# Attention products of a run kept together on TensorE, products with v issued for two pieces at a time

## The chip, the cores and the metric

One core of one Trainium2 chip runs the program. The metric is the device time of one launch in microseconds (us); the kernel before was run three times, with 1156.73, 1160.39 and 1160.76 us, median 1160.39. Engines are named as in the profile: PE is TensorE, DVE VectorE, ACT ScalarE, POOL GpSimd, SP SyncE.

## What is computed

Sigmoid attention over 8 batches of 12 heads (448 positions, head dimension 64), and then a two-layer network on the 3584 tokens. Cut to what matters:

```python
scores = q @ k.T / sqrt(64) - log(448)
attn = 1 / (1 + exp(-scores))
x = attn @ v                       # heads side by side: 3584 x 768
h = x @ w_in                       # 768 -> 2048
g = where(h >= 1, h, where(h <= -1, 0, (h + 1)**2 / 4))
out = g @ w_out                    # 2048 -> 768
```

## The kernel before

The data are 32-bit floats. From the ninth pair of heads on, q and k are written as a high and a low half in 16 bits (`hl`, made in `prep_b`), from the fifteenth on v and the attention weights too (`v`, `ahl`), and each product of two such operands is the sum of three 16-bit matmuls: high by high, and the two mixed ones. The weights of the network and its activations are split in the same way.

**Attention.** Two heads form a pair (`p`), and a pair has four pieces (`c`): three blocks of 128 key positions and a last one, the middle piece, with the 64 that are left, in which both heads lie side by side. A piece `i = 4 p + c` goes through four steps:

- `scores` (line 387) makes the piece's scores in a PSUM tile `psc`, of which there are two. Per head one matmul over all 128 rows of the array takes the high half of q and both halves of k (line 409), and one over 64 rows adds the low half of q (line 418). The two matmuls of line 418, one per head, use the upper and the lower half of the array's rows. A middle piece from pair 14 on takes three whole-array matmuls instead (line 404).
- `weigh` applies the sigmoid on ACT in PSUM (line 450), copies the high half out on ACT (line 458) and makes the low half on DVE (line 459). The `psc` tile is free after that.
- `av` (line 466) multiplies with v into `pav` (line 491): six matmuls for a whole piece, four for a middle one. Each gives 64 rows of output, head 0 in the left and head 1 in the right half of the array's columns, and the two heads alternate.
- After a pair's last piece ACT copies `pav` to x (line 500), and DVE takes its largest value (line 501).

In the column of one-row sums, `all_sum` (line 155) adds up the largest values of a later pair in a matmul with 2 or 3 columns; what comes out sets that pair's scales, with which `prep_b` splits it on POOL.

**Network.** For the first two batches the first layer is line 719; from the third on it runs in a block scheme with seven products instead of eight (`up_blocks`, line 685), 128x224 each. The second layer is line 755 for all. During the second batch DVE and ACT also make the weights of the block scheme (`mix` and `unmixed`, lines 625 to 653).

**Order.** `step(i)` issues the scores up to piece `i + 3` and then `av`; up to pair 13 it takes one piece a step, from pair 14 on two pieces every second step. The main loop calls `step` between the units of the network of the batch before, so that attention of batch b + 1 runs within the network of batch b. Inside that, a list scheduler at build time orders each engine's instructions by priority and by when it reckons their operands to be there: the order on PE is not the order of the calls. PE runs it strictly in that order.

At the end of a batch `start_blocks` and `finish_blocks` take the largest x of all (DVE, one PE matmul in line 171, DVE) and split x; the next batch's first layer waits for that.

Of the kernel before, what the change touches and what calls it, by code (L numbers as in the profile page):

```python
# [14 lines left out]
F32 = mybir.dt.float32  # L15
# [3 lines left out]
AF = mybir.ActivationFunctionType  # L19
ALU = mybir.AluOpType  # L20
# [3 lines left out]
P = 128  # L24
# [29 lines left out]
QA = 17  # L54
QT = 3
CORN = 10
TP = 1

DW = 8
# [10 lines left out]
def sigmoid_attention_mlp(ctx: ExitStack, tc: tile.TileContext, first_qvk, qkv, w_in, w_out, out_t):  # L70
# [312 lines left out]

    pieces = {}

    def scores(todo):

        tiles = []
        for i in todo:
            p, c = divmod(i, NPC)  # L390
            mid = c == NKC
            w = slice(c * P, S if mid else (c + 1) * P)
            psc = ps_sc.tile([P, 2, 512], F32, tag="psc", name="psc")
            tiles.append(psc)
            if p < NFULL:
                r = ready[p][0]
                for j in range(2):
                    out = psc[j * D : (j + 1) * D, 0, :S] if mid else psc[:, j, :S]
                    rows = slice(j * D, (j + 1) * D)
                    nc.tensor.matmul(out, r[rows, 2, w], r[rows, 0, :], start=True, stop=True)  # L400
            elif mid and p >= NFULL + NHALF:
                hl = ready[p][4]
                for t, (kh, qh) in enumerate(((0, 0), (1, 0), (0, 1))):
                    nc.tensor.matmul(psc[:, 0, :S], corner(p)[:, kh, :], hl[:, 0, qh, :], start=t == 0, stop=t == 2)  # L404
            else:
                kq = ready[p][0]
                for j in range(2):
                    out = psc[j * D : (j + 1) * D, 0, :S] if mid else psc[:, j, :S]
                    nc.tensor.matmul(out, kq[:, j, 1, w], kq[:, j, 0, :], start=True, stop=False)  # L409
        for i, psc in zip(todo, tiles):  # L410
            p, c = divmod(i, NPC)
            mid = c == NKC
            if p >= NFULL and not (mid and p >= NFULL + NHALF):
                hl, w = ready[p][4], slice(c * P, S if mid else (c + 1) * P)
                for j in range(2):
# [22 lines left out]
    def weigh(i, psc):  # L438
# [5 lines left out]
        sqk = 1.0 / math.sqrt(D) if p < NFULL else ready[p][2][:, 0:1]  # L444
        if p < NFULL + NHALF:
            a32 = att_p.tile([P, 2, S], F32, tag="ahl", name="a32")
            nc.scalar.activation(a32[:, :n, :], a, AF.Sigmoid, bias=nls, scale=sqk)  # L447
# [8 lines left out]
            parts = [(a, ahl[:, 0], ahl[:, 1])]  # L456
        for x, hi, lo in parts:
            nc.scalar.activation(hi, x, AF.Copy, scale=ATT)  # L458
            nc.vector.scalar_tensor_tensor(out=lo, in0=x, scalar=ATT, in1=hi, op0=ALU.mult, op1=ALU.subtract)  # L459
        pieces[i] = ahl  # L460

    state = {"scored": 0}

    def av(i):
        p, c = divmod(i, NPC)
        b, hp = divmod(p, NP)
        if c == 0:
            state["pav"] = ps_av.tile([P, 512], F32, tag="pav", name="pav")
            if hp == 0:
                state["xm"] = sml_p.tile([P, NP], F32, tag="xm", name="xm", bufs=2)  # L470
        pav = state["pav"]
        at = pieces.pop(i)
        mid = c == NKC
        v = ready[p][1]
        split = p >= NFULL + NHALF
        terms = []
        for j in range(2):
            o = slice(j * D, (j + 1) * D)
            full_v = slice((2 * c + j) * D, (2 * c + j + 1) * D)
            if p < NFULL and mid:  # L480
                full_v = slice(2 * c * D, (2 * c + 1) * D)
            if not split:
                r = o if mid else slice(0, P)
                terms.append([(v[r, full_v], at[r, 0 if mid else j, :])])
            elif mid:
                terms.append([(v[:, vh, full_v], at[:, 0, j, :]) for vh in range(2)])
            else:
                terms.append([(v[:, vh, full_v], at[:, ah, j, :]) for vh, ah in ((0, 0), (1, 0), (0, 1))])
        for t in range(len(terms[0])):
            for j in range(2):  # L490
                nc.tensor.matmul(  # L491
                    pav[j * D : (j + 1) * D, :S], *terms[j][t],
                    start=c == 0 and t == 0, stop=mid and t == len(terms[j]) - 1,
                )
# [296 lines left out]
    def step(i):  # L791
# [6 lines left out]
        if c == 2:  # L798
            prep_b(p + 2)
            if late:  # L800
                prep_a(p + 3)
        if i < NPC * (NFULL + NHALF):
# [12 lines left out]


    wi = Weight(w_in, w_in_sb, "wi", [5 + 2 * (f % 6) for f in range(NFC)])
# [152 lines left out]
```

## Time and profile before

| | |
|---|---|
| median of 3 runs | 1160.39 us |
| the profiled execution, as timed | 1159.12 us |
| its span in the trace | 1157.4 us |
| PE matmul busy | 1135.0 us, 98% of the span |
| PE weight loads | 666.1 us, 58%, beside the matmuls |
| DVE busy | 815.8 us, 70% |
| ACT busy | 722.1 us, 62% |
| POOL busy | 294.4 us, 25% |
| mean granted TensorE clock | 0.999 of full speed |

The span is from the first to the last instruction; the launch around it adds 1.7 us. A matmul counts as busy from its start to its modelled end, which lies behind the start of the next one. Where matmuls follow each other closely the time that one costs is therefore read as the distance between two starts, from the timeline, and not from its duration.

### The profile page before, as it was taken

The page shows a single profiled execution, that of the slowest core. Times are in us where ns is not written, and L with a number is a line of the kernel's source. Part 1 is how long each engine was busy: PE and PEld are TensorE (multiplying, and loading weights), DVE is VectorE, ACT ScalarE, POOL GpSimd, SP SyncE. Part 2 cuts the span into 40 slices and gives each one's busy share as a digit, 9 for nine tenths or more (in the row PEclk, how much of TensorE's full clock was granted, in tenths as well). Part 3 has the DMA queues.
Part 4 walks back from the last instruction along what each step waited for, and adds up shares of the span by engine and source line. Part 5 has one row for each costly group of instructions (what it writes and reads, how often), then busy time and mean ns, then how long its engine had stood idle before and what let it go on. Part 6 is the DMA issues. An engine that isn't in the chain of part 4 may idle for free.

```text
span 1157.4 us, 20215 instructions
## 1 busy us (share of the span) xinstructions
PE 1135.0 (98%) x7662; PEld 666.1 (58%) x7662; DVE 815.8 (70%) x1730; ACT 722.1 (62%) x1199; POOL 294.4 (25%) x367
## 2 busy tenths in 40 slices
PE   8899999999999999999999999999999999999998
PEld 2234334444446775567745785457854677558954
DVE  6988886879987895468936787367964589646820
ACT  6978888578666784557754786447764576423410
POOL 0000000001542354324523353325344233210000
PEclk9999999999999999999999999999999999999999
DMA  9943443162564654225632465224742165203300
GB/s 366 380 138 135 143 165 97 50 212 105 192 209 144 239 211 127 76 94 205 219 102 65 145 207 203 66 66 147 264 145 76 53 207 200 100 17 123 133 22 27
DMA packets 58112, 170.00 MB, mean 147 GB/s; under 512 B 8608, under 2 KB 39840, under 8 KB 51872
## 3 DMA queue, kind: packets, MB, share of 16 engines
q1 hardware_dynamic: 56288, 159.29, 39.9%
q10 hardware_dynamic: 1728, 9.44, 2.3%
q8 instruction: 60, 0.98, 0.3%
q14 instruction: 36, 0.29, 0.1%
HBM read 126.94 MB, written 23.40 MB: 130 GB/s over the span
## 4 chain that ended last, share of the span: by engine, by line
PE 76%; DMA 8%; DVE 6%; ACT 4%; POOL 3%; issue 1%; SPq 0%; POOLq 0%; DVEq 0%; ACTq 0%
PE po L755 30%; PE ph L685 23%; PE pav L491 8%; PE ph L719 7%; DMA raw<-qkv 4%; PE psc L409 3%; PE psc L418 3%; DMA w_out_sb<-w_in 2%; PE psc L404 1%; DVE ahl L459 1%; ACT psc L450 1%; POOL hl L373 1%; DVE mixa L625 1%; ACT dump L335 1%; POOL raw L371 1%
## 5 line engine op out<-in xcount | busy, mean ns | idle before, releaser
L755 PE MATMUL po<-ghl,w_out_sb 128*128 128x448 f16 x2304 | 446.9, 353 | 1.8 <-ACT ghl L735 1.8
L755 PEld LDWEIGHTS <-w_out_sb 128*128 128x128 f16 x2304 | 221.5, 98 | 217.2 <-issue 17.6
L685 PE MATMUL ph<-w_in_sb 128*128 128x224 f16 x3024 | 307.7, 259 | 1.7 <-DMA w_in_sb<-blocks 1.3
L685 PEld LDWEIGHTS <-w_in_sb 128*128 128x128 f16 x3024 | 282.6, 98 | 31.1 <-issue 27.6
L459 DVE SCALAR_TENSOR_TENSOR ahl<-psc,ahl 128x896 f16<-128x896 f32 (+1 forms) x170 | 153.0, 900 | 98.8 <-ACT ahl L458 96.9
L450 ACT ACTIVATE psc<-psc,nls,sqk 128x896 f32<-128x896 f32 (+1 forms) x136 | 129.8, 971 | 94.0 <-PE psc L418 76.1
L371 POOL TENSOR_SCALAR raw<-raw,qkv_s 128x448 f32<-128x448 f32 (+1 forms) x93 | 70.9, 777 | 443.8 <-DVE qkv_i L135 355.7
L458 ACT ACTIVATE ahl<-psc 128x896 f16<-128x896 f32 (+1 forms) x170 | 127.0, 762 | 30.6 <-DVE ahl L459 29.4
L719 PE MATMUL ph<-xhl,w_in_sb 128*128 128x448 f16 x576 | 112.5, 353 | 0.0
L335 ACT ACTIVATE dump<-raw 128x448 f16<-128x448 f32 (+1 forms) x105 | 61.6, 587 | 72.0 <-DMA raw<-qkv 71.3
L694 DVE TENSOR_TENSOR xhl<-ph,xhl 128x224 f32<-128x224 f32 x240 | 87.7, 383 | 26.0 <-PE ph L685 19.6
L491 PE MATMUL pav<-ahl,v 128*64 128x448 f16 x748 | 98.2, 360 | 0.4 <-DVE ahl L459 0.4
L735 ACT ACTIVATE ghl<-g 128x448 f16<-128x448 f32 x128 | 72.5, 572 | 37.2 <-DVE g L734 36.7
L732 ACT ACTIVATE g<-xhl,hr,ihr 128x448 f32<-128x448 f32 x96 | 68.7, 752 | 41.8 <-DVE xhl L694 40.8
L736 DVE TENSOR_TENSOR ghl<-g,ghl 128x448 f16<-128x448 f32 x128 | 84.2, 664 | 8.2 <-ACT ghl L735 7.7
L733 DVE SCALAR_TENSOR_TENSOR g<-g,rk 128x448 f32<-128x448 f32 x112 | 79.8, 727 | 13.9 <-ACT g L732 13.5
L719 PEld LDWEIGHTS <-w_in_sb 128*128 128x128 f16 x576 | 54.8, 98 | 58.2 <-issue 8.9
L373 POOL TENSOR_TENSOR hl<-raw,hl 128x448 f16<-128x448 f32 x62 | 72.8, 1194 | 0.0
L409 PE MATMUL psc<-qk 128*128 128x448 f16 x252 | 66.4, 354 | 2.8 <-ACT a L447 1.8
L734 DVE SCALAR_TENSOR_TENSOR g<-xhl,ihs,g 128x448 f32<-128x448 f32 x96 | 66.3, 708 | 0.3
L768 DVE TENSOR_SCALAR o<-po,od 128x448 f32<-128x448 f32 x42 | 28.5, 679 | 53.1 <-PE po L755 53.1
L430 POOL COPY w_in_sb<-hl 64x128 f16<-64x128 f16 x68 | 32.4, 476 | 127.3 <-DVE hl L367 125.4
(151 smaller groups left out, 1131.6 us busy)
## 6 DMA issues: line engine op xcount, KB each, us to landing
w_in_sb<-blocks SPq DMA_DIRECT2D x48, 1344.0 KB, 6.6
raw<-qkv SPq DMA_DIRECT2D x34, 704.0 KB, 4.8
qk<-hl SPq DMA_DIRECT2D x320, 56.0 KB, 2.0
w_out_sb<-w_in SPq DMA_DIRECT2D x16, 768.0 KB, 11.1
out_t<-o SPq DMA_DIRECT2D x48, 224.0 KB, 1.9
blocks<-mixs SPq DMA_DIRECT2D x8, 768.0 KB, 3.5
w_out_sb<-w_out ACTq DMA_DIRECT2D x6, 768.0 KB, 4.6
raww<-w_out ACTq DMA_DIRECT2D x6, 768.0 KB, 5.8
```

The source lines that it names most:

```text
L371: nc.gpsimd.tensor_scalar(out=rt, in0=rt, scalar1=s[:, t : t + 1], scalar2=1.0, op0=ALU.mult, op1=ALU.mult)
L373: nc.gpsimd.tensor_tensor(out=dst[:, 1, :], in0=rt, in1=hi, op=ALU.subtract)
L409: nc.tensor.matmul(out, kq[:, j, 1, w], kq[:, j, 0, :], start=True, stop=False)
L450: nc.scalar.activation(a, a, AF.Sigmoid, bias=nls, scale=sqk)
L458: nc.scalar.activation(hi, x, AF.Copy, scale=ATT)
L459: nc.vector.scalar_tensor_tensor(out=lo, in0=x, scalar=ATT, in1=hi, op0=ALU.mult, op1=ALU.subtract)
L491: nc.tensor.matmul(pav[j * D : (j + 1) * D, :S], *terms[j][t], start=c == 0 and t == 0, stop=mid and t == len(terms[j]) - 1,)
L685: nc.tensor.matmul(out, w[:, wt, wh, c * P : (c + 1) * P], xc[:, xt, c, xh, :], start=j in (0, 2) and c + wh + xh == 0, stop=c == HC - 1 a ...
L694: add = lambda out, q, other: nc.vector.tensor_tensor(out=out, in0=quarter(q), in1=other, op=ALU.add)
L719: nc.tensor.matmul(ph[:, :S], w_in_sb[:, f, wh, c * P : (c + 1) * P], xhl[:, c, xh, :], start=c == 0 and wh + xh == 0, stop=c == NCC - 1 a ...
L736: (nc.gpsimd if f % GPOOL else nc.vector).tensor_tensor(out=ghl[:, f, 1, :], in0=g, in1=hi, op=ALU.subtract)
L755: nc.tensor.matmul(po[:, :S], w_out_sb[:, f, wh, m * P : (m + 1) * P], ghl[:, f, gh, :], start=f == lo and wh + gh == 0, stop=f == hi - 1 ...
```

## The change

- `chain` gives each run of attention matmuls a handler: the first is issued as before, each further one at a priority raised by 600 and in program order behind what was issued. A run is the line 409 matmuls of a piece, its line 418 matmuls, the three of line 404, and all those of one `av` call.
- `av` takes the list of pieces of a step (two from pair 14 on) and makes one run of them: 12 matmuls for two whole pieces, 10 with a middle one. `when_made` hangs a semaphore wait for the low halves of both pieces on the first matmul of the run.
- Line 409 takes head 1 before head 0.
- The `all_sum` of a later pair is issued between the whole-array score matmuls and those of line 418; before it came after the latter.

No matmul, activation, vector operation or transfer is added or taken away. The diff, cut (indentation inside `av` changed throughout):

```diff
+GROUPED = 14
+RUN_PRIO = 600
...
+    def when_made(some):
+        waits = [ins for i in some if i >= NPC * GROUPED for ins in made.get(i, ())]
+        def once(ins):
+            while waits:
+                tc.add_manual_dep(
+                    ins.ins, waits.pop().ins.name,
+                    mybir.DependencyInfo(mybir.DependencyClass.Sync, mybir.DependencyReason.DATA), reason="group",
+                )
+            return ins
+        return once
+
+    def chain():
+        begun = []
+        def run(issue):
+            if not begun:
+                begun.append(issue())
+                return
+            with tc.high_priority(offset=RUN_PRIO):
+                tc.keep_in_program_order(issue())
+        return run
...
+            run = chain()
             if p < NFULL:
...
-                    nc.tensor.matmul(out, r[rows, 2, w], r[rows, 0, :], start=True, stop=True)
+                    run(lambda: nc.tensor.matmul(out, r[rows, 2, w], r[rows, 0, :], start=True, stop=True))
...
-                for j in range(2):
+                for j in (1, 0):
...
+        for i, psc in zip(todo, tiles):
+            p, c = divmod(i, NPC)
+            if c == NKC and p >= NFULL + NHALF and p + 2 in maxes:
+                sums[p + 2] = all_sum(maxes[p + 2], 3, psc[:, 1, :])
...
-                    nc.tensor.matmul(out, hl[rows, 1, 0, w], hl[rows, 0, 1, :], start=False, stop=True)
-            if mid and p >= NFULL + NHALF and p + 2 in maxes:
-                sums[p + 2] = all_sum(maxes[p + 2], 3, psc[:, 1, :])
+                    run(lambda: nc.tensor.matmul(out, hl[rows, 1, 0, w], hl[rows, 0, 1, :], start=False, stop=True))
...
-            nc.vector.scalar_tensor_tensor(out=lo, in0=x, scalar=ATT, in1=hi, op0=ALU.mult, op1=ALU.subtract)
+            made.setdefault(i, []).append(nc.vector.scalar_tensor_tensor(
+                out=lo, in0=x, scalar=ATT, in1=hi, op0=ALU.mult, op1=ALU.subtract
+            ))
...
-    def av(i):
-        p, c = divmod(i, NPC)
+    def av(some):
+        once, run = when_made(some), chain()
+        for i in some:
+            p, c = divmod(i, NPC)
...
-                nc.tensor.matmul(
+                    run(lambda: once(nc.tensor.matmul(
...
-        for k in some:
-            av(k)
+        av(some)
```

What the scheduler makes of it on PE is seen at two places of the fourth batch's network, the first at 551 us of the trace. In the rows, `psc` is a piece's score tile, `hl` the halves of q and k, `ph` the first layer's sums; each LDWEIGHTS loads the operand of the MATMUL under it. A piece's two low score matmuls before, the first:

```order
L409 LDWEIGHTS qk_5620
L409 MATMUL psc_6049<-qk_5620 128x448
L418 LDWEIGHTS hl_5609
L418 MATMUL psc_6049<-hl_5609 128x448
L685 LDWEIGHTS w_in_sb_90
L685 MATMUL ph_5962<-w_in_sb_90 128x224
```

and the second, after 18 matmuls of line 685:

```order
L685 MATMUL ph_5962<-w_in_sb_90 128x224
L418 LDWEIGHTS hl_5609
L418 MATMUL psc_6049<-hl_5609 128x448
L685 LDWEIGHTS w_in_sb_90
L685 MATMUL ph_5873<-w_in_sb_90 128x224
```

With the change (lines 409, 418 and 685 are now 443, 458 and 727) both stand behind those 18:

```order
L727 MATMUL ph_5962<-w_in_sb_90 128x224
L458 LDWEIGHTS hl_5609
L458 MATMUL psc_6049<-hl_5609 128x448
L458 LDWEIGHTS hl_5609
L458 MATMUL psc_6049<-hl_5609 128x448
L727 LDWEIGHTS w_in_sb_90
L727 MATMUL ph_5873<-w_in_sb_90 128x224
```

The two halves of the array's rows are now filled by neighbours.

The second place, some 90 matmuls on, is the run of products with v into `pav_6071` (`mb` and `one` are the operands of a one-row sum). Before, after five of the run's twelve:

```order
L491 LDWEIGHTS v_5610
L491 MATMUL pav_6071<-ahl_5930,v_5610 64x448
L155 LDWEIGHTS one_96
L155 MATMUL psc_6052<-mb_6058,one_96 128x3
L491 LDWEIGHTS v_5610
L491 MATMUL pav_6071<-ahl_5930,v_5610 64x448
```

With the change (lines 491 and 155 are now 533 and 157), behind the twelfth:

```order
L533 LDWEIGHTS v_5610
L533 MATMUL pav_6071<-ahl_5934,v_5610 64x448
L157 LDWEIGHTS one_96
L157 MATMUL psc_6052<-mb_6056,one_96 128x3
L727 LDWEIGHTS w_in_sb_90
L727 MATMUL ph_5962<-w_in_sb_90 128x224
```

The sum no longer parts the run.

The third place is on DVE, at the end of the second batch, between the last largest value of x (line 501) and the diagonal matrix (line 161) that the matmul of line 171 waits for. `mixa` is a stage of the block weights. Before:

```order
L625 TENSOR_TENSOR mixa<-w_in_sb 128x768 x2
L501 TENSOR_REDUCE xm<-x_92 128x1
L536 TENSOR_TENSOR xhl<-x_92,xhl 128x672
L629 TENSOR_TENSOR mixa<-mixa 128x384
L523 TENSOR_REDUCE xm_3283<-xm 128x1
L459 SCALAR_TENSOR_TENSOR ahl<-psc,ahl 128x896
L630 SCALAR_TENSOR_TENSOR mixa<-mixa,mixes 128x384
L161 TENSOR_SCALAR diag<-ident,xm_3283 128x128
```

With the change:

```order
L543 TENSOR_REDUCE xm<-x_92 128x1
L578 TENSOR_TENSOR xhl<-x_92,xhl 128x672
L565 TENSOR_REDUCE xm_3283<-xm 128x1
L163 TENSOR_SCALAR diag<-ident,xm_3283 128x128
L667 TENSOR_TENSOR mixa<-w_in_sb 128x768 x2
L496 SCALAR_TENSOR_TENSOR ahl<-psc,ahl 128x896
L671 TENSOR_TENSOR mixa<-mixa 128x384
```

The block weights of line 625 (now 667) and what follows from them have moved behind the diagonal matrix. On PE, 35 matmuls of line 755 stand between the batch's last product with v and the matmul of line 171 with the change, 56 before, with one piece's scores ahead of the 35.

## Rows read from the trace of the kernel before

**Rows 1.** The page's head: span; busy time, share of the span and instructions of each engine; TensorE's granted clock in 40 slices of the span, in tenths of full speed.

```profile
span 1157.4 us, 20215 instructions
...
PE 1135.0 (98%) x7662; PEld 666.1 (58%) x7662; DVE 815.8 (70%) x1730; ACT 722.1 (62%) x1199; POOL 294.4 (25%) x367
...
PEclk9999999999999999999999999999999999999999
```

**Rows 2.** Waits of PE from 250 us to the end: engine, line, what it waited for; us in total, times, longest.

```profile
PE psc L171 <- DVE diag L161: 2.1, 1, 2.1
PE po L755 <- ACT ghl L735: 1.8, 3, 1.1
...
PE pav L491 <- DVE ahl L459: 0.4, 1, 0.4
...
PE psc L404 <- DVE ahl L459: 0.2, 1, 0.2
```

**Rows 3.** Groups of PE instructions by line and shape over the whole span: rows*columns of the array, output, count; busy us and mean ns of one; idle time ahead of them.

```profile
L755 PE MATMUL po<-ghl,w_out_sb 128*128 128x448 f16 x2304 | 446.9, 353 | 1.8 <-ACT ghl L735 1.8
...
L491 PE MATMUL pav<-ahl,v 128*64 128x448 f16 x748 | 98.2, 360 | 0.4 <-DVE ahl L459 0.4
L409 PE MATMUL psc<-qk 128*128 128x448 f16 x240 | 64.2, 353 | 2.6 <-ACT a L447 1.6 <-DMA qk<-hl 0.6 <-issue 0.3
L418 PE MATMUL psc<-hl 64*128 64x448 f16 x240 | 44.3, 358 | 0.0
```

**Rows 4.** Timeline of PE in the fourth batch's network: start us, us from the first start to the last end, line, operands, rows*columns of the array, count of the run.

```profile
550.78 0.54 PE L409 MATMUL psc<-qk 128*128 128x448 f16 x2
551.25 0.36 PE L418 MATMUL psc<-hl 64*128 64x448 f16 x1
551.54 1.90 PE L685 MATMUL ph<-w_in_sb 128*128 128x224 f16 x18
553.37 0.36 PE L418 MATMUL psc<-hl 64*128 64x448 f16 x1
553.66 3.62 PE L685 MATMUL ph<-w_in_sb 128*128 128x224 f16 x36
557.13 0.73 PE L404 MATMUL psc<-hl,w_in_sb 128*128 128x448 f16 x3
557.79 0.75 PE L491 MATMUL pav<-ahl,v 128*64 128x448 f16 x5
558.47 0.18 PE L155 MATMUL psc<-mb,one 128*128 128x3 bf16 x1
558.58 0.94 PE L491 MATMUL pav<-ahl,v 128*64 128x448 f16 x7
559.46 4.49 PE L685 MATMUL ph<-w_in_sb 128*128 128x224 f16 x45
```

**Rows 5.** The same view a little later, where the scheduler had kept two pieces together by itself.

```profile
589.47 0.55 PE L418 MATMUL psc<-hl 64*128 64x448 f16 x4
589.95 1.14 PE L491 MATMUL pav<-ahl,v 128*64 128x448 f16 x10
591.02 8.12 PE L755 MATMUL po<-ghl,w_out_sb 128*128 128x448 f16 x42
598.97 0.54 PE L409 MATMUL psc<-qk 128*128 128x448 f16 x2
```

**Rows 6.** Busy time by stretch: from:to us, length, then busy us and count of PE, PEld, DVE, ACT and POOL, granted clock, DMA share, GB/s.

```profile
280.00:340.00 60.00, 59.34 (x324) 27.30 (x324) 52.87 (x85) 46.23 (x75) 26.96 (x30) 1.00 0.48 170
...
620.00:680.00 60.00, 60.00 (x488) 42.52 (x487) 42.84 (x109) 39.82 (x68) 17.78 (x23) 1.00 0.40 137
...
955.00:985.00 30.00, 28.85 (x253) 21.45 (x252) 27.87 (x59) 20.61 (x34) 12.17 (x15) 1.00 0.58 207
```

**Rows 7.** Timelines of DVE and of PE around 296 us, in the second batch's network; in brackets idle time ahead of the row, and what ended it.

```profile
291.84 3.62 DVE L625 TENSOR_TENSOR mixa<-w_in_sb 128x768 f32<-128x768 f16 x2
295.38 1.08 DVE L459 SCALAR_TENSOR_TENSOR ahl<-psc,ahl 128x896 f16<-128x896 f32 x1
...
296.51 0.73 PE L404 MATMUL psc<-hl,w_in_sb 128*128 128x448 f16 x3 [0.23 <-DVE ahl L459]
```

**Rows 8.** One piece of the fourth batch's network from its scores to its product with v, out of the timelines of ACT, DVE and PE.

```profile
564.66 1.07 ACT L450 ACTIVATE psc<-psc,nls,sqk 128x896 f32<-128x896 f32 x1 [1.34 <-PE psc L418]
567.52 0.90 ACT L458 ACTIVATE ahl<-psc 128x896 f16<-128x896 f32 x1
...
570.21 1.08 DVE L459 SCALAR_TENSOR_TENSOR ahl<-psc,ahl 128x896 f16<-128x896 f32 x1
575.35 1.08 DVE L459 SCALAR_TENSOR_TENSOR ahl<-psc,ahl 128x896 f16<-128x896 f32 x1
...
577.47 0.57 PE L491 MATMUL pav<-ahl,v 128*64 128x448 f16 x4
```

**Rows 9.** Timeline of PE at the end of the second batch, from the last product with v to the matmul of line 171.

```profile
331.06 0.57 PE L491 MATMUL pav<-ahl,v 128*64 128x448 f16 x3
331.56 10.77 PE L755 MATMUL po<-ghl,w_out_sb 128*128 128x448 f16 x56
344.41 0.23 PE L171 MATMUL psc<-diag,one 128*128 128x128 bf16 x1 [2.08 <-DVE diag L161]
```

More of the change, by code (lines that the diff above doesn't have):

```diff
@@ L384, in sigmoid_attention_mlp @@
     pieces = {}
+    made = {}
+    def when_made(some):
[17 more added lines that the diff above has]
+        return run
     def scores(todo):
@@ L403, in scores @@
                 for t, (kh, qh) in enumerate(((0, 0), (1, 0), (0, 1))):
[L404 removed]
+                    run(lambda: nc.tensor.matmul(
+                        psc[:, 0, :S], corner(p)[:, kh, :], hl[:, 0, qh, :], start=t == 0, stop=t == 2
+                    ))
             else:
                 kq = ready[p][0]
[L407 removed]
+                for j in (1, 0):
                     out = psc[j * D : (j + 1) * D, 0, :S] if mid else psc[:, j, :S]
[L409 removed]
+                    run(lambda: nc.tensor.matmul(out, kq[:, j, 1, w], kq[:, j, 0, :], start=True, stop=False))
+        for i, psc in zip(todo, tiles):
+            p, c = divmod(i, NPC)
+            if c == NKC and p >= NFULL + NHALF and p + 2 in maxes:
+                sums[p + 2] = all_sum(maxes[p + 2], 3, psc[:, 1, :])
         for i, psc in zip(todo, tiles):
@@ L414, in scores @@
                 hl, w = ready[p][4], slice(c * P, S if mid else (c + 1) * P)
+                run = chain()
                 for j in range(2):
@@ L446, in weigh @@
             a32 = att_p.tile([P, 2, S], F32, tag="ahl", name="a32")
-            nc.scalar.activation(a32[:, :n, :], a, AF.Sigmoid, bias=nls, scale=sqk)
+            made[i] = [nc.scalar.activation(a32[:, :n, :], a, AF.Sigmoid, bias=nls, scale=sqk)]
             pieces[i] = a32
@@ L458, in weigh @@
             nc.scalar.activation(hi, x, AF.Copy, scale=ATT)
-            nc.vector.scalar_tensor_tensor(out=lo, in0=x, scalar=ATT, in1=hi, op0=ALU.mult, op1=ALU.subtract)
+            made.setdefault(i, []).append(nc.vector.scalar_tensor_tensor(
+                out=lo, in0=x, scalar=ATT, in1=hi, op0=ALU.mult, op1=ALU.subtract
+            ))
         pieces[i] = ahl
     state = {"scored": 0}
-    def av(i):
-        p, c = divmod(i, NPC)
[L466 to L489, printed above, removed]
-            for j in range(2):
-                nc.tensor.matmul(
-                    pav[j * D : (j + 1) * D, :S], *terms[j][t],
-                    start=c == 0 and t == 0, stop=mid and t == len(terms[j]) - 1,
-                )
@@ new lines, in av @@
+    def av(some):
+        once, run = when_made(some), chain()
+        for i in some:
+            p, c = divmod(i, NPC)
+            b, hp = divmod(p, NP)
+            if c == 0:
+                state["pav"] = ps_av.tile([P, 512], F32, tag="pav", name="pav")
+                if hp == 0:
+                    state["xm"] = sml_p.tile([P, NP], F32, tag="xm", name="xm", bufs=2)
+            pav = state["pav"]
+            at = pieces.pop(i)
+            mid = c == NKC
+            v = ready[p][1]
+            split = p >= NFULL + NHALF
+            terms = []
+            for j in range(2):
+                o = slice(j * D, (j + 1) * D)
+                full_v = slice((2 * c + j) * D, (2 * c + j + 1) * D)
+                if p < NFULL and mid:
+                    full_v = slice(2 * c * D, (2 * c + 1) * D)
+                if not split:
+                    r = o if mid else slice(0, P)
+                    terms.append([(v[r, full_v], at[r, 0 if mid else j, :])])
+                elif mid:
+                    terms.append([(v[:, vh, full_v], at[:, 0, j, :]) for vh in range(2)])
+                else:
+                    terms.append([(v[:, vh, full_v], at[:, ah, j, :]) for vh, ah in ((0, 0), (1, 0), (0, 1))])
+            for t in range(len(terms[0])):
+                for j in range(2):
+                    run(lambda: once(nc.tensor.matmul(
+                        pav[j * D : (j + 1) * D, :S], *terms[j][t],
+                        start=c == 0 and t == 0, stop=mid and t == len(terms[j]) - 1,
+                    )))
```

2 lines of the change are left out of this document (1 added, 1 removed).

## The prediction, made before the changed kernel was run

> **What bounds the kernel.** I read the page's head first: PE is busy for 1135.0 of 1157.4 us, 98%, and its clock stands at full speed in all 40 slices [rows 1]. The table of PE's waits comes next: from 250 us on its longest are 2.1 us for DVE at a batch's end and 1.8 us for activations, and products with v waited for a low half once, 0.4 us [rows 2]. So PE is the bound, and time is won only by giving it less to do between two starts. The groups by line say where to look: 2304 second-layer matmuls take 446.9 us, 194 ns each. The 748 products with v take 98.2 us, 131 ns each, though two of them, one per half of the array's columns, should share one passage; the 240 low score products take 44.3 us, 185 ns each [rows 3]. The timeline tells why, read by the distances between starts.
>
> - A matmul of 448 columns holds the array for 0.189 us: 42 of line 755 take 7.95 us, 591.02 to 598.97 [rows 5]. One of 224 columns: 36 in 3.47 us, 0.096 us [rows 4].
> - Two neighbours that use different halves share that time: from the first of ten products with v to the next matmul it is 1.07 us [rows 5], five passages (0.947) and 0.12 us over; ten passages would be 1.89.
> - The time over recurs wherever the part of the array that matmuls use changes (whole, half of the columns, half of the rows), and nowhere else: two of line 409 to line 418 0.47 us, two passages and 0.09; one of line 418 to line 685 0.29, one passage and 0.10; 18 of line 685 to line 418 1.83, 0.10 over; seven products with v to line 685 0.88, four passages and 0.12 [rows 4]; four of line 418 to the products with v 0.48, two passages and 0.10 [rows 5]. Line 685 to line 404, whole array to whole array, costs nothing over: the 3.47 us above [rows 4]. I take **0.10 us for a change of form**.
> - A run of an odd number leaves half a passage unused: the twelve products that the one-row sum parts into 5 and 7 take three and four passages, not six, and so do two low score products that stand apart [rows 4].
>
> A page of the Trainium skill speaks against these passages: "TensorE: Matmul & The Clock Gate", section "Back-to-back issue gap", says that in a stream of weight loads and matmuls 512 columns cost about 131 ns each, because neighbours are pipelined. Scaled to 448 columns (an estimate from that page) a passage would cost 0.115 us, the second term below would be 3.9 us in place of 6.4, and the time 2.5 us more. The trace does not agree with the page: 0.189 us [rows 5] holds over 42 in a row.
>
> **The change, part by part.** It adds and removes no operation, so its worth is the order on PE. I counted it over all 7486 matmuls of both programs.
>
> 1. *Changes of form*: 515 before, 408 after. 107 x 0.10 = **10.7 us**. Of these 19 fall in each of four batches of the block scheme, 7 before the second batch ends its first layer, 11 in its second layer, 13 in the rest.
> 2. *Odd runs*: 48 of products with v and 20 of low score products before, none after. Two of them cost one passage: 34 x 0.189 = **6.4 us**.
> 3. *The 32-bit pairs* (the first 14): their runs stand as they did, 57 changes of form up to the first layer's start in both. Nothing.
> 4. *Head 1 before head 0* in line 409, and the priorities themselves: same matmuls, same form, nothing. What they do to the order is in 1 and 2.
> 5. *The sum of a later pair* moves by a run at most. Behind it stands POOL's split, which is no bound: POOL is busy for 25% [rows 1]. From each such sum to that pair's first score matmul the order has at least 20 us of matmuls in the 16-bit part, as before. Nothing; without that cover the next pair's scores would wait.
> 6. *The wait for two pieces*. A run now starts when the later piece's low half is there, and behind its first matmul all of PE stands. In the block batches a piece gets its scores, then ACT 1.07 and 0.90 us and DVE 1.08 us; with queues it is ready at 571.29 and its partner at 576.43, and the products begin at 577.47 [rows 8]. So 1.0 us is left with both waited for, where the run starts at the old time. After the change runs begin no earlier behind their scores: the least distance from a piece's last score product to its first product with v rises from 6.8 to 8.3 us of matmuls. No cost there.
> 7. *Where DVE is the narrow place*. From 280 to 340 us, while block weights are made, DVE is busy for 52.87 of 60 us, and from 955 to 985 for 27.87 of 30; in a block batch's middle it is 42.84 of 60 [rows 6]. At 296.51 a middle piece's scores start just 0.05 us after DVE freed the score tile (295.38 + 1.08 = 296.46), behind two block-weight operations of 3.62 us [rows 7]. The new order puts these scores some 2 us of matmuls earlier, since the products with v that stood ahead are gone to other places; DVE will not be 2 us earlier, so PE waits. The same comparison, scores by scores, gives less than that at the other tight places of the two stretches, and one wait shifts all that follows and pays for its neighbours. From below: PE's waits after 250 us can't shrink by more than their largest few, some 4 us [rows 2]. From above: half of the gain, 9 us, if each tight place of both stretches pays in full and some more appear. I take **3 us lost**, nearest to the 2 us at 296 with 1 us for the later stretch.
> 8. *The batch's end*. The matmul of line 171 came 13.35 us after the last products with v, 10.77 of them filled by 56 matmuls, then 2.08 us idle [rows 9]. Now 35 matmuls fill it, 4 us less, but on DVE the block-weight work that stood ahead of the diagonal matrix is behind it: two operations of line 625 alone took 3.62 us at the other place [rows 7]. I let the two cancel.
>
> Sum: 10.7 + 6.4 - 3 = 14.1 us. The profiled execution took 1159.12 us, so 1145.0; it lies 1.27 us under the median of the three runs, 1160.39. Against that median: **1146.3 us**, 1.2% less.
>
> **Rivals.**
> - *Nothing is given back*: DVE's new order also relieves 280 to 340 us. Then 17.1 us less, 1143.3; with the wait at the batch's end gone too, 1141. For it: the least distance from scores to products grew. Against: rows 7, tight to 0.05 us. Chance 0.25.
> - *The narrow places eat half*: a place like that of rows 7, at 2 us, in four batches instead of one, 17.1 - 8 = 9.1 us less, 1151.3. "TensorEngine Tiling (Array Packing)", section "PSUM Bottleneck", in the Trainium skill says as much: tiling speeds TensorE up, not the emptying of PSUM, which may bound next. In this kernel that means the two score tiles, each held until DVE's low half: in the stretch of rows 7 they are the bound, in the block batches DVE has 17 of 60 us free [rows 6]. Chance 0.14.
> - *The drain is elsewhere*: the 0.10 us at a change of form overlaps with something that a longer run then shows, so that grouping moves it and saves nothing: 6.4 - 3 = 3.4 us less, 1157.0. Against it: the run of ten pays it once at either end, 0.10 and 0.12, and nothing within [rows 5]. Chance 0.03.
> - *The pair wait turns into a stall of each run*, and it is slower. 68 runs of 16-bit products now begin with a wait for the later low half; in strict order PE stands behind it. At 17.1 / 68 = 0.25 us each the gain is gone; the nearest row, the one wait of this kind, is 0.4 us [rows 2], which would give 68 x 0.4 - 17.1 = 10 us more, 1170. Against it: 1.0 us of room in rows 8, where the pair is late, and all but five or so places have more. Chance 0.03.
>
> **How the numbers follow.** The forecast (1 to 5 us given back) has 0.55, the rivals 0.25, 0.14, 0.03 and 0.03. The range 1140.5 to 1153 takes in the first three, and the two ends of item 7. What a measurement of this kernel can tell from no change is about 0.5%, 5.8 us: all of the first three lie beyond it, apart from the edge of the half-eaten case (0.01). Faster by more 0.93, the same 0.04, slower 0.03.
>
> **What would show it.** The products with v in 16 bits should fall from 98.2 us to about 84 (34 runs of ten at 1.14 us [rows 5], 34 of twelve at a passage more), the low score products by 3 or so, with unchanged means and counts. The timeline should have runs of 10 and 12 products with v without a one-row sum inside, ending 5 or 6 passages and 0.1 us after their start, and low score products in twos and fours. PE's waits should gain 2 to 4 us for DVE line 459 (now 496) between 280 and 340 us, in scores rather than products with v. It is wrong if the distances at a change of form are not 0.10 us in the new trace, or if the products with v wait for low halves in many runs.

## The result: slower by 0.7%, with PE's work cut as forecast

The changed kernel took 1167.41 us, the median of 5 runs (1166.08 to 1169.62); the kernel before took 1160.76 beside it (1156.73 to 1161.12). The ratio is 1.0067, with a 95% interval of 1.0046 to 1.0087. The forecast was 1146.3 us, range 1140.5 to 1153. Read the new profile in the order of the old one: the head of the page first (its lines answer to [rows 1]).

```profile
span 1165.4 us, 20217 instructions
...
PE 1124.0 (96%) x7662; PEld 670.0 (57%) x7662; DVE 820.0 (70%) x1730; ACT 723.3 (62%) x1199; POOL 295.6 (25%) x367
...
PEclk9999999999999999999999999999999999999999
```

PE is busy for 11.0 us less, so the change does give it less to do. But the span is 8.0 us longer: PE's idle time has grown from 22.4 to 41.4 us, by 19.0. The groups by line tell what was saved. They answer to [rows 3], with the same columns.

```profile
L797 PE MATMUL po<-ghl,w_out_sb 128*128 128x448 f16 x2304 | 451.9, 355 | 10.7 <-ACT ghl L777 10.2 <-ACT w_out_sb L279 0.5
...
L533 PE MATMUL pav<-ahl,v 128*64 128x448 f16 x748 | 83.7, 357 | 2.3 <-DVE ahl L496 2.3
L443 PE MATMUL psc<-qk 128*128 128x448 f16 x240 | 62.8, 353 | 2.6 <-ACT a L484 1.4 <-PE ph L727 0.6 <-DVE ahl L496 0.4
L458 PE MATMUL psc<-hl 64*128 64x448 f16 x240 | 41.1, 358 | 0.0
```

Products with v fell from 98.2 to 83.7 us (forecast: about 84), low score products from 44.3 to 41.1 (forecast: 3 less), with the counts as before and means within 3 ns. The table of PE's waits from 250 us on, which answers to [rows 2], has where it went.

```profile
PE po L797 <- ACT ghl L777: 10.2, 4, 2.9
PE ph L727 <- DVE xhl L736: 8.6, 7, 2.6
PE pav L533 <- DVE ahl L496: 2.3, 2, 1.3
PE ph L761 <- DVE g L776: 2.1, 1, 2.1
...
PE psc L436 <- DVE ahl L496: 0.8, 1, 0.8
```

The wait that the change adds, of products with v for low halves, is the third row: 2.3 us in all. The large rows are two others. The second layer waits for its activations, 10.2 us in four places against 1.8 in three before (0.20, 1.13 and 0.45); the first layer, in the block scheme, waits for the sums that DVE takes out of PSUM, 8.6 us against 0.4 before. The row of before, from the same table:

```profile
PE ph L685 <- DVE xhl L694: 0.4, 1, 0.4
```

**One of the four places.** In the rows `ghl` is an activation of the network as 16-bit halves, which the second layer multiplies, and `raw` the q, k and v of a pair as they come from memory. PE's timeline with the change, at the end of the first layer of the third batch's network:

```profile
418.70 1.33 PE L533 MATMUL pav<-ahl,v 128*64 128x448 f16 x12
419.96 0.18 PE L157 MATMUL psc<-mb,one 128*128 128x3 bf16 x1
419.99 4.47 PE L727 MATMUL ph<-w_in_sb 128*128 128x224 f16 x45
...
424.78 0.36 PE L458 MATMUL psc<-hl 64*128 64x448 f16 x2
425.07 1.90 PE L727 MATMUL ph<-w_in_sb 128*128 128x224 f16 x18
...
429.52 1.30 PE L797 MATMUL po<-ghl,w_out_sb 128*128 128x448 f16 x6
430.65 1.89 PE L727 MATMUL ph<-w_in_sb 128*128 128x224 f16 x18
...
440.00 2.07 PE L797 MATMUL po<-ghl,w_out_sb 128*128 128x448 f16 x10
444.53 3.94 PE L797 MATMUL po<-ghl,w_out_sb 128*128 128x448 f16 x20 [2.46 <-ACT ghl L777]
```

The grouping is as foreseen: twelve products with v in 1.26 us from start to start, six passages and 0.13; two low score products in 0.29, one passage and 0.10. Now the same place before, PE and then ACT:

```profile
420.84 0.18 PE L155 MATMUL psc<-mb,one 128*128 128x3 bf16 x1
...
431.67 3.76 PE L755 MATMUL po<-ghl,w_out_sb 128*128 128x448 f16 x19
435.26 1.89 PE L685 MATMUL ph<-w_in_sb 128*128 128x224 f16 x18
...
441.89 5.47 PE L755 MATMUL po<-ghl,w_out_sb 128*128 128x448 f16 x28
447.56 0.73 PE L755 MATMUL po<-ghl,w_out_sb 128*128 128x448 f16 x3 [0.20 <-ACT ghl L735]
...
443.00 0.58 ACT L335 ACTIVATE dump<-raw 128x448 f16<-128x448 f32 x1 [3.15 <-DMA raw<-qkv]
...
446.94 0.57 ACT L735 ACTIVATE ghl<-g 128x448 f16<-128x448 f32 x1
```

From the one-row sum to the first matmul of the second layer that needs the first layer's last block PE had 26.5 us of work before (420.84 to 447.36, where its 0.20 us of idle time begins) and now has 22.1 (419.96 to 442.07). The first layer's last 18 matmuls come behind 6 second-layer ones instead of 19, and 42 instead of 58 second-layer matmuls stand ahead of the first that needs the last block. So of the 4.4 us that are missing, 3.0 (16 x 0.189) are not saved: these matmuls still run, but behind the place where PE waits. It is so in all four places: 36 second-layer matmuls follow the wait now, and 20 followed it before in the three places that had one. What must happen in that time is on three other engines, with the change:

```profile
427.45 2.64 POOL L373 TENSOR_SCALAR raw<-raw,qkv_s 128x448 f32<-128x448 f32 x3 [10.24 <-ACT g L774]
...
436.67 0.59 SPq L383 DMA_DIRECT2D qk<-hl  x1
437.37 0.53 SPq L321 DMA_DIRECT2D raw<-qkv  x1
...
435.00 1.42 ACT L774 ACTIVATE g<-xhl,hr,ihr 128x448 f32<-128x448 f32 x2 [1.00 <-DVE xhl L736]
442.32 0.58 ACT L337 ACTIVATE dump<-raw 128x448 f16<-128x448 f32 x1 [5.90 <-DMA raw<-qkv]
442.80 0.19 ACT L337 ACTIVATION_READ_ACCUMULATOR dump<-raw 128x1 f32 x1
442.89 0.56 ACT L777 ACTIVATE ghl<-g 128x448 f16<-128x448 f32 x1
...
443.92 0.56 ACT L777 ACTIVATE ghl<-g 128x448 f16<-128x448 f32 x1
```

The one-row sum at 419.96 gives the scales of one pair. POOL splits that pair from 427.45 on. SP moves its halves, and only then, in strict order, issues the transfer of a later pair's q, k and v at 437.37. (That transfer also writes into the buffer that POOL's split reads, one of two; the split's last operation ends at 436.61, so SP's queue holds it 0.65 us longer than the buffer does.) ACT takes that pair's row measures from it (line 337, `dump<-raw`) and stands before them for 5.90 us, until 442.32. Behind them in ACT's queue are the two `ghl` of the network's last block, which the next matmul on PE needs; it starts when the second has ended, at 444.48.

Before, the transfer came as late (row measures at 443.00, after 3.15 us idle) and the second `ghl` even later, at 446.94, but PE came 5.3 us later too. The chain hardly moves when PE gets faster (from the one-row sum to the row measures 22.2 us before and 22.4 now), since the time in it belongs to DVE's queue, POOL, SP and the transfer. The Trainium skill has the rule behind it ("PSUM — Partial Sum Buffer", section "Engine vs sequencer instructions": the queues of ScalarE, VectorE and GpSimdE are strict first in, first out); the trace agrees, with `ghl` at 442.89, 0.09 us after the read of the first row measure began.

**TensorE's clock.** Near these places the granted clock fell. By the stretches (columns as in [rows 6]):

```profile
582.40:585.81 3.41, 3.21 (x9) 1.31 (x9) 1.01 (x3) 3.41 (x7) 0.00 (x0) 0.50 0.01 3
585.81:589.30 3.49, 3.49 (x20) 1.78 (x19) 3.24 (x8) 0.72 (x2) 0.00 (x0) 1.00 0.11 41
```

For 3.41 us it stood at 0.50 (1.2 of 2.4 GHz), and nine matmuls ran where the next 3.49 us, at full clock, held 20. PE was at the end of a wait of 2.72 us. The same happened at 722.4, 862.3 and 985.2; before the change no stretch inside the run shows it (mean clock 0.999, now 0.994). By execution the mean is 0.997 to 1.000 in twenty of the kernel before and 0.991 to 0.994 in the five of the change. Four times 3.41 us at half speed cost some 6.8 us, an estimate at half of that time. They count as busy time: three of the four lie in matmuls of line 797, whose group rose from 446.9 to 451.9 us.

**The narrow places** of [rows 6], with the change:

```profile
280.00:340.00 60.00, 54.38 (x309) 25.63 (x308) 52.96 (x89) 45.46 (x72) 25.36 (x28) 1.00 0.40 144
620.00:680.00 60.00, 60.00 (x493) 43.27 (x492) 44.60 (x111) 38.63 (x66) 18.35 (x23) 1.00 0.35 121
955.00:985.00 30.00, 24.58 (x228) 19.62 (x226) 25.20 (x49) 19.07 (x33) 9.43 (x11) 1.00 0.59 219
```

From 280 to 340 us PE now idles for 5.62 us instead of 0.66, from 955 to 985 for 5.42 instead of 1.15. But in the later stretch DVE, too, is busy for less, 25.20 us instead of 27.87: its timeline and PE's show it standing before a transfer.

```profile
961.35 1.68 DVE L341 TENSOR_REDUCE m<-raw 128x2 f32<-128x896 f32 x2 [3.46 <-DMA raw<-qkv]
...
966.30 1.89 PE L727 MATMUL ph<-w_in_sb 128*128 128x224 f16 x18 [2.61 <-DVE xhl L736]
```

This stretch holds 4.2 of the 8.6 us that the first layer waits for DVE's sums. The other 4.4 lie elsewhere, and most of them stay when the transfers come earlier (run 1 below): in the first layer of each of four batches PE waits some 1.1 us (1.09, 1.06, 1.19 and 1.10), where the table of before has no such wait. The first of them:

```profile
414.59 3.61 PE L727 MATMUL ph<-w_in_sb 128*128 128x224 f16 x36 [1.09 <-DVE xhl L736]
```

### The profile page after: what moved, and what is told of

It is laid out like the page before. It is cut to its first block, busy times and chain, and to the rows that moved or that the text cites. A ratio compares the mean times of both kernels' runs of the same rounds, so it can differ in the third digit from the quotient of the medians.

```text
span 1165.4 us, 20217 instructions
## 1 busy us (share of the span) xinstructions
PE 1124.0 (96%) x7662; PEld 670.0 (57%) x7662; DVE 820.0 (70%) x1730; ACT 723.3 (62%) x1199; POOL 295.6 (25%) x367
## 4 chain that ended last, share of the span: by engine, by line
PE 65%; DVE 14%; ACT 6%; DMA 5%; POOL 4%; issue 4%; SPq 1%; POOLq 0%; ACTq 0%; DVEq 0%
PE po L797 31%; PE ph L727 14%; PE ph L761 7%; PE pav L533 6%; DMA raw<-qkv 4%; DVE ahl L496 3%; PE psc L443 3%; DVE g L775 2%; DVE g L776 2%; DVE xhl L736 2%; PE psc L458 2%; POOL hl L375 2%; DVE ghl L778 1%; POOL raw L373 1%; DMA w_out_sb<-w_in 1%
## 5 line engine op out<-in xcount | busy, mean ns | idle before, releaser
L797 PE MATMUL po<-ghl,w_out_sb 128*128 128x448 f16 x2304 | 451.9, 355 | 10.7 <-ACT ghl L777 10.2
L727 PEld LDWEIGHTS <-w_in_sb 128*128 128x128 f16 x3024 | 285.7, 98 | 33.0 <-issue 26.5
L778 DVE TENSOR_TENSOR ghl<-g,ghl 128x448 f16<-128x448 f32 x128 | 85.8, 677 | 23.1 <-ACT ghl L777 22.7
L775 DVE SCALAR_TENSOR_TENSOR g<-g,rk 128x448 f32<-128x448 f32 x112 | 85.2, 774 | 9.2 <-ACT g L774 8.8
L533 PE MATMUL pav<-ahl,v 128*64 128x448 f16 x748 | 83.7, 357 | 2.3 <-DVE ahl L496 2.3
L776 DVE SCALAR_TENSOR_TENSOR g<-xhl,ihs,g 128x448 f32<-128x448 f32 x96 | 72.0, 770 | 0.2
```

What stands on the lines that cost most here:

```text
L533: run(lambda: once(nc.tensor.matmul(pav[j * D : (j + 1) * D, :S], *terms[j][t], start=c == 0 and t == 0, stop=mid and t == len(terms[j]) - ...
L727: nc.tensor.matmul(out, w[:, wt, wh, c * P : (c + 1) * P], xc[:, xt, c, xh, :], start=j in (0, 2) and c + wh + xh == 0, stop=c == HC - 1 a ...
L775: nc.vector.scalar_tensor_tensor(out=g, in0=g, scalar=rt, in1=g, op0=ALU.min, op1=ALU.mult)
L778: (nc.gpsimd if f % GPOOL else nc.vector).tensor_tensor(out=ghl[:, f, 1, :], in0=g, in1=hi, op=ALU.subtract)
L797: nc.tensor.matmul(po[:, :S], w_out_sb[:, f, wh, m * P : (m + 1) * P], ghl[:, f, gh, :], start=f == lo and wh + gh == 0, stop=f == hi - 1 ...
```

## The experiments

**Theory 1:** PE's saved time is lost where ACT and DVE, in strict order, stand before a pair's transfer, and in the falls of the clock that PE's waits there bring. **Theory 2:** the change costs the time by itself, through the wait for two pieces, the raised priorities or the scores' order. Each run is compared with the kernel before as it ran beside it; its median was 1160.06 for the first four, 1159.74 for the next four and 1161.34 for the last two. "PE's work by counts" prices each change of form at 0.096 us and each passage lost to an odd run at 0.189.

**1. Transfers earlier, in the change.** Two more buffers, in a space that other tiles shared, let a pair's transfer go out one pair earlier from the 23rd pair on.

```diff
+SPARE0 = 20
-        raws[p] = raw_p.tile([P, 2 * S + VW], F32, tag="raw", name="raw")
+        if p >= SPARE0 and p % 2:
+            raws[p] = raw_p.tile([P, 2 * DM], I32, tag="raww", name="raw").bitcast(F32)[:, : 2 * S + VW]
+        else:
+            raws[p] = raw_p.tile([P, 2 * S + VW], F32, tag="raw", name="raw")
...
         if c == 0:
             load_pair(p + 3)
+            if p + 4 >= SPARE0 + 2:
+                load_pair(p + 4)
             prep_a(p + 2)
```

> The change, with four buffers instead of two for the raw q, k, v of a pair (odd pairs from 21 on use the two buffers of the block weights, idle by then), and each pair's transfer issued one pair earlier. The order on PE is that of the change but for one matmul, the order on ACT the same up to the last batches. Theory 1 (the time that PE saves is lost where ACT and DVE, in strict order, stand before a pair's largest values that wait for its transfer, with the network's activations behind them): PE's waits for line 777 of the change fall from 10.2 us to under 2, the falls of the clock behind them (four of 3.4 us at half speed, 6.8 us) mostly go, the 2.6 us at 966 go: 1148 to 1153 us. Theory 2 (the wait for two pieces and the raised priority themselves stall PE, or load DVE and ACT at bad times): no transfer matters, 1165 to 1168 us.

Measured: **1144.28 us** (1143.66 to 1144.41), ratio 0.9867, interval 0.9849 to 0.9885; clock 1.000. It is below both kernels and even below theory 1's range. PE's order is the same up to the 2320th matmul and differs at 258 of 7486 places in all. The longest waits of PE from 250 us on:

```profile
PE ph L731 <- DVE xhl L740: 3.8, 6, 1.2
PE ph L765 <- DVE g L780: 2.1, 1, 2.1
PE pav L537 <- DVE ahl L500: 1.9, 2, 1.0
```

The wait for `ghl` is gone, and of that for DVE's sums 3.8 us are left, mostly in the four batches named above:

```profile
414.91 3.61 PE L731 MATMUL ph<-w_in_sb 128*128 128x224 f16 x36 [1.16 <-DVE xhl L740]
```

At the place shown above, ACT and PE:

```profile
437.40 0.58 ACT L341 ACTIVATE dump<-raw 128x448 f16<-128x448 f32 x1 [0.72 <-DVE ghl L782]
...
439.44 0.56 ACT L781 ACTIVATE ghl<-g 128x448 f16<-128x448 f32 x1
...
440.46 0.56 ACT L781 ACTIVATE ghl<-g 128x448 f16<-128x448 f32 x1
...
440.32 8.12 PE L801 MATMUL po<-ghl,w_out_sb 128*128 128x448 f16 x42
```

The second `ghl` now starts at 440.46 instead of 443.92, and 42 second-layer matmuls run without a gap, though the one-row sum stands within 0.4 us of where it stood (420.28). POOL's split (427.72) and SP's issue of a transfer (437.64) are within 0.3 us of theirs too; only the transfer issued there is one that nobody waits for yet. From 955 to 985 us PE is busy for 30.00 us of 30. From 280 to 340 us, where no transfer was moved, it is busy for 54.41 us of 60, as in the change.

**2. The same in the kernel before.**

> The same earlier transfers in the kernel before, whose PE order stays as it was but for a few matmuls (520 changes of form instead of 515). PE there waits some 2 us in all for what stands behind these transfers. Theory 1: 1157 to 1160 us, so that the change is worth 8 us or more with early transfers in both. Theory 2: 1157 to 1160 us too, and the change still loses 7 us against it.

Measured: 1158.09 us (1157.58 to 1159.58), ratio 0.9985 (0.9973 to 0.9997). Early transfers alone are worth 2.0 us there and 23.1 in the change. With them the change is worth 1158.09 - 1144.28 = **13.8 us**; the forecast had 14.1.

**3. The change without the wait for two pieces.**

```diff
-        waits = [ins for i in some if i >= NPC * GROUPED for ins in made.get(i, ())]
+        waits = []
```

> The change without the wait for two pieces (when_made hangs nothing on the first matmul). The built order then keeps fewer runs: 533 changes of form, PE matmul work as before the change (by count times distance 1 us less than before, 16 more than with the change). Theory 1: with the PE work of before the waits of before return, 1157 to 1162 us, PE's waits for activations under 4 us. Theory 2: if the wait for two pieces is what costs, PE's waits fall as well, but by the 2.3 us that products with v wait in the change: 1176 to 1182 us, since the work rises by 16 us.

Measured: 1163.77 us (1160.97 to 1167.65), ratio 1.0034 (1.0022 to 1.0047). Theory 2 is far off; theory 1's range is missed by 1.8 us, and why was not followed. PE is busy for 1137.3 us: without that wait the scheduler parts the runs again, and nothing is saved.

**4. Runs of products with v and their wait alone,** scores and the one-row sum as before.

```diff
-            run = chain()
+            run = lambda issue: issue()
...
-                for j in (1, 0):
+                for j in range(2):
```

> Products with v in runs with the wait for two pieces, scores and one-row sums as before the change. 422 changes of form (408 with the change, 515 before); the first second-layer matmul that needs the last block of the first layer stands 13.0 us of matmuls behind that block in four batches (9.6 with the change, 10.3 before). Theory 1: PE comes later to that matmul, its wait there goes, 1147 to 1155 us. Theory 2 (the wait for two pieces costs): it is still in, 1163 to 1168 us. If the raised priority of the scores is what hurts, as theory 1.

Measured: 1152.74 us (1151.66 to 1153.62), ratio 0.9945 (0.9925 to 0.9966). In theory 1's range, but half of the 15.2 us is lost. PE's waits from 250 us on include 4.3 us in which scores wait for DVE's low halves (0.93 us in each of four batches), 2.4 for one of DVE's sums and 2.3 of products with v.

**5. The scores' half alone,** with `av([k])` for each piece, no run and no wait.

> The change's other half by itself: the scores keep together (head 1 first, sum of a later pair between whole-array and low score matmuls), the products with v are issued as in the kernel before, with no wait for two pieces. Transfers of pairs as they were. The order has 471 changes of form instead of 515 and 14 passages fewer lost to odd runs: 44 x 0.096 + 14 x 0.189 = 6.9 us less work for PE. 59 second-layer matmuls stand ahead of the first that needs a batch's last block, as before (58), so theory 1 (the saved time is lost where ACT stands before a pair's transfer while PE arrives earlier) expects little of it lost: 1152 to 1157 us. Rival, theory 2 in its other form (the scores' order itself costs the time): 1160 to 1166.

Measured: 1153.35 us (1150.85 to 1156.06), ratio 0.9943 (0.9922 to 0.9964), 6.4 us less. So each half makes the kernel faster, by 7.3 and 6.4 us, and both together make it slower. At the place shown above, this half keeps PE's work between the one-row sum and the first matmul on the last block at 26.3 us (419.49 to 445.79; 26.5 before, 22.1 with the change), and PE waits there for 0.47 us. PE's work as a whole is 6.9 us less, so what costs at that place is not the saving itself but how early PE arrives there, and most of that is order.

**6 to 8. The parts with early transfers** (the edits of 4, 5 and 3, each with that of 1; only in run 6 the transfer goes out at the pair's third piece and not its first, so half a pair earlier and not a whole one).

> Runs of products with v and their wait for two pieces, scores as before, and the transfers of pairs from the 23rd on one pair earlier (the buffers of the run with early transfers). 426 changes of form: PE's work by counts is 15.2 us less than in the kernel before with early transfers (1158.09 us). Theory 1 (nothing else costs time once the transfers are there): 1142 to 1147 us. Theory 2 (the wait for two pieces has a price of its own, hidden by what the early transfers gave): 1150 or more.

> Scores kept together, products with v as before, transfers of pairs from the 23rd on one pair earlier. 475 changes of form: PE's work by counts is 7.2 us less than in the kernel before with early transfers (1158.09 us). Theory 1: 1149 to 1153 us. Theory 2 in its other form (the scores' order costs): 1156 to 1162.

> The whole change without the wait for two pieces, transfers of pairs from the 23rd on one pair earlier. Without that wait the scheduler parts the runs again: 545 changes of form, PE's work by counts 0.5 us less than in the kernel before with early transfers (1158.09 us). Theory 1 (PE's work alone decides once the transfers are early): 1155 to 1161 us, so that the wait for two pieces is worth some 14 us. Theory 2 (the wait for two pieces costs): no slower than the changed kernel with early transfers, 1144 or less.

Measured: 1147.56 us (1146.45 to 1148.58), ratio 0.9891 (0.9866 to 0.9916), 0.6 us above theory 1's range; 1151.40 (1150.79 to 1151.80), ratio 0.9924 (0.9904 to 0.9944); 1159.40 (1158.03 to 1160.81), ratio 0.9997 (0.9983 to 1.0010). All five pairs together (with early transfers the counts shift by at most 1.1 us):

| version | PE's work by counts | transfers as they were | transfers early | gain |
|---|---|---|---|---|
| before | 0 | 1160.06 | 1158.09 | 2.0 |
| change, no wait for two pieces | -1.0 | 1163.77 | 1159.40 | 4.4 |
| scores' half | -6.9 | 1153.35 | 1151.40 | 2.0 |
| products with v's half | -15.2 | 1152.74 | 1147.56 | 5.2 |
| change | -16.7 | 1167.41 | 1144.28 | 23.1 |

With early transfers the times order themselves by PE's work, all but the first two, which lie within 1.3 us of each other. Theory 2 falls as the cause of the slowdown: between the change and the change without the wait for two pieces, both with early transfers, that wait, with the runs that hang on it, *saves* 15.1 us. A smaller price does survive early transfers. Run 6 keeps 10.5 of its 15.2 us; in each of four batches its scores wait 0.93 us until DVE has made a low half, as in run 4, most of this row:

```profile
PE psc L447 <- DVE ahl L497: 4.1, 5, 0.9
```

The whole change keeps 13.8 of 16.7 us, with the waits of run 1.

**9. ACT and DVE without the wait, transfers left where they were.** The measures from the 19th pair on are taken of x instead of the transfer's data.

```diff
+            rx = raws[p] if p < RES0 else x32.rearrange("p h s -> p (h s)")[:, : 2 * S + VW]
...
-                    rt = raws[p][:, t * S : 2 * S + VW if t == 2 else (t + 1) * S]
+                    rt = rx[:, t * S : 2 * S + VW if t == 2 else (t + 1) * S]
```

> The change, but from the 19th pair on the largest values are taken of x (same shape, already on the chip) instead of the pair's q, k and v, so that ACT and DVE do the same work without waiting for the pair's transfer; this leaves out the right scales. The transfers, and POOL's split behind them, stay where they are in the change. The order has 415 changes of form and 0.7 us more PE work by counts than the change; 42 second-layer matmuls still stand ahead of the first that needs a batch's last block. Theory 1 (it is ACT and DVE, standing in strict order before the transfer, that hold PE back): the four waits of 2.5 to 2.9 us for ghl and the falls of the clock behind them are gone, 1143 to 1150 us. Rival: it is the later split or the order of PE itself that holds PE back, then the time stays above 1160.

Measured: **1149.79 us** (1148.92 to 1150.24), ratio 0.9901 (0.9886 to 0.9915). The transfer is still issued and still lands 4.9 us later, POOL still splits behind it; only ACT and DVE no longer read it. PE's wait for `ghl` is gone from 250 us on, and the longest that are left there are others:

```profile
PE ph L729 <- DMA w_in_sb<-blocks: 3.4, 4, 1.4
PE psc L174 <- DVE diag L164: 2.6, 1, 2.6
```

**10. The same in the kernel before.**

> The same edit in the kernel before: from the 19th pair on the largest values are taken of x instead of q, k and v, which leaves out the right scales. Its order falls out with 492 changes of form instead of 515 and 4.8 us less PE work by counts. Theory 1: in the kernel before the waits of ACT cost PE next to nothing, so only the count shows, 1153 to 1157 us. Rival (the waits cost the kernel before as much as the changed one, some 20 us): 1135 to 1142.

Measured: 1151.56 us (1150.64 to 1152.43), ratio 0.9914 (0.9898 to 0.9931): 9.8 us less, of which 4.8 are counted work. It lies 1.4 us below theory 1's range, and 9.6 above the rival's. Of the other 5 us, 3.7 are PE's waits from 250 us on, which fall from 6.9 to 3.2. But with this edit in both kernels the change is worth only 1.8 us (1151.56 to 1149.79), where PE's work by counts is 11.2 us apart: PE's waits from 250 us on are 11.2 us in run 9, among them the two shown, and 3.2 in run 10. So run 9 shows that the waits for `ghl` come from the row measures that stand before the transfer; it does not show that the saving is whole once they are gone. This edit moves the order more than the early transfers do, so the pair 1 and 2 is the cleaner one.

## Why the prediction was wrong

- **Steps 1 and 2 (changes of form, odd runs), 17.1 us.** Right in mechanism and size: the groups of lines 533 and 458 fell by 14.5 and 3.2 us, and the distances in the timeline are as read. Step 4 cost nothing in experiment 5, which has the scores' order as a gain; step 3 was not tested by itself.
- **Step 5 (the one-row sum of a later pair) failed.** It put the chain behind that sum at nothing. It asked only whether that pair's *own* scores would wait, and called POOL no bound at 25% busy. The consumer that counted is another: POOL's split ends, SP's queue comes free, the *next* transfer goes out, and ACT and DVE stand before it in strict order with the network's activations behind them. The cover to ask for was the 26.5 us to the first second-layer matmul on the last block. It was used up before the change: PE waited there for 0.20 us, and in two later batches for 1.13 and 0.45, which are the 1.8 us of [rows 2] (a total of three waits, which the prediction read as one of the longest). The change took 4.4 us off this cover, 3.0 of them by order alone, and PE's wait became 2.10 to 2.95 us in each of four batches: 10.2 us for `ghl`, 4.2 more behind the transfer at 961 us, and 6.8 in the clock. The row that shows it, 3.15 us of ACT idle for the transfer, was not among those read.
- **Step 6 (wait for two pieces).** Right for products with v, which wait in no block batch; two waits, 2.3 us in all, fall in the stretch of step 7. But "no cost there" missed the first layer's wait of 1.1 us for DVE's sums in each of four block batches, 4.4 us; early transfers leave most of it. Why DVE comes late there was not followed.
- **Step 7 (where DVE is narrow), 3 us.** Mis-sized in one stretch and mistaken in the other. From 280 to 340 us idle time rose by 5.0 us, in products with v (2.3) more than in scores (1.2) and, for 2.1 us, in the first layer. From 955 to 985 it rose by 4.3, but not because DVE was full: DVE stood before the transfer, and with early transfers nothing is lost there.
- **Step 8 (the batch's end).** Better than forecast: the wait of [rows 9], 2.08 us, has left the table and nothing stands in its place. With the 5.0 us just before it that makes 2.9 lost, close to the 3 of step 7 by luck.
- **The clock** was in no step, and what would become of it if PE began to wait was not asked. 6.8 us. The line of 40 slices in [rows 1] can't show such a fall: 3.41 us at half speed take 6% off a slice of 29 us, a 9 stands for 90% or more, and the changed kernel has forty of them too. The mean clock shows it.
- **The sum.** 23.1 us lie between the change with late and with early transfers. The rows account for 10.2 of them in the wait for `ghl`, which is gone, 4.8 in that for DVE's sums (8.6 to 3.8) and 6.8 in the clock; 1.3 are not placed. With early transfers the span is 1142.6 us; the forecast, 1145.0 for the profiled execution less the 1.7 around it, was 1143.3. That it comes so near is in part luck. Beside the kernel before with early transfers PE is busy for 20.4 us less (1136.7 to 1116.3; 1.7 of them are a fall of the clock in the profile of run 2) and idle for 6.9 us more (19.4 to 26.3), where the forecast had 17.1 saved and 3 given back.
- **The rivals.** The one that ended slower, at 1170 us, came near the time and had the wrong cause: it had each run of products with v stall, and they waited 2.3 us in all. "The narrow places eat half" had the right form, a small place paid once in every batch, with two score tiles for the cause instead of a transfer. Its score tiles are seen in runs 4 and 6, 0.93 us in each of four batches, and not in those batches of the change.

## What to carry to other kernels

Before forecasting a gain on the engine that bounds, list for each batch the chains that run beside it through other engines and end in it, and their slack at its current speed: a wait of 0.2 us there says that the slack is used up, and time saved ahead of that point, or work that a new order moves behind it, comes back as a wait. Count the work between where the chain starts and where it ends, not only the total. Look for idle time on the other engines that ends with a transfer, however little those engines are busy; what stands behind it in the queue, and not what it feeds, may be what hurts. When a change that cuts the bounding engine's work comes out slower, try it again with the new wait removed before it is given up: here that was worth 23.1 us, and the kernel at **1144.28 us** is 1.3% faster than the one before.

## What the runs showed of the hardware

Waits of a few microseconds cost more than themselves. TensorE's granted clock fell from 2.4 to 1.2 GHz for 3.41 us at the end of waits of 2.72 and 2.95 us (at 582.4 and 722.4), 0.8 us after the end of one of 2.10 (at 862.3), and at 985.2 behind 0.31, 0.64 and 1.25 us of waits within some 4 us. It did not fall after 2.46 us at 444.53 nor after 2.61 us at 966.30, so the length of the wait alone does not tell. Nor do the waits just ahead: PE waits 0.95, 0.75 and 1.31 us between 50 and 59 us in run 2, 0.95, 0.75 and 1.32 there in the kernel before, and the clock fell in run 2 (at 58.07, for 3.41 us) and not in the kernel before. What decides it stays open. No experiment took a fall of the clock away and left its wait by design.
